# Turning q and k of two batches by DMA transfers, sine tables at the start, and a new order, in a fused attention and gated-convolution kernel

## The chip, the cores and the metric

The kernel runs on one core of one Trainium2 chip. The metric is the device time of one execution in microseconds; for the kernel before it is 174.66 us, the median of three runs (173.97, 174.66, 174.69). A profile of one execution shows the engines: PE is TensorE (matmuls; PEld its weight loads), DVE VectorE, ACT ScalarE, POOL GpSimd, SP SyncE. POOL and SP mainly issue DMA transfers here.

## The reference

Two blocks run one after the other on 4 batches, 8 heads, 768 positions and 64 values per head. The first is attention in which a query sees the 96 latest keys and the first 8, with a bias that grows with distance; the second takes its output as x.

```python
scores = scale * np.matmul(q, k.transpose(0, 1, 3, 2))
is_global = pos[None, :] < 8
is_local = (rel >= 0) & (rel < 96)
bias = -slopes[:, None, None] * dist[None, :, :]
scores = np.where(is_global | is_local, scores + bias, -1e9)
a = softmax(scores)                      # over the keys
x = np.matmul(a, v)                      # then (batch, seq, 512)

proj = x @ w_proj                        # 512 -> 3 * 512
x1, x2, x3 = split(proj)
X2 = np.fft.rfft(x2, n=S, axis=1)
H = np.fft.rfft(filter_fft, n=S, axis=0)
x2_conv = np.fft.irfft(X2 * H, n=S, axis=1)
out = (x1 * x2_conv * x3) @ w_out
```

## The kernel before

Attention of one batch has 7 key tiles of 128 rows (8 global keys and 120 others) and 6 query tiles of 128 rows, each row holding all 8 heads (512 values, fp16). The loads give q and k with positions on the partitions (`qn`, `kn`); the score matmuls need the head's 64 values on the partitions, so every tile is turned: `turned` (line 633) does four 128x128 transposes on PE per tile (line 640) into a PSUM bank and one copy out of it (line 306, on ACT or DVE) into `QT` or `KT`. Batches 1 to 3 turn two tiles per bank, batch 0 one; batch 0's queries are turned from fp32 by `turned32` (line 621). There is one `qn`, one `kn`, one `QT` and one `KT` for all batches. `v` has two buffers.

Work on keys goes in three groups, `GRP` = tiles (0,1), (2,3), (4,5,6), called c0 to c2. For each group and each pair of heads `scores` (line 658, matmuls in line 680) writes PSUM, ACT takes the exp (line 694), and from batch 1 on DVE multiplies a mask (line 711). `values` (lines 729 and 734) multiplies by v, DVE normalises (line 753), `transpose_x` (line 774) turns the result, and `gate` (line 843) makes x1 and x3.

`conv` does the rest of the second block: projections to x2 (line 910), a Fourier transform written as matmuls (line 614) with sine tables `fwd`, the product with the filter's spectrum on DVE, the inverse transform (line 935 and 938) and the output matmul (line 962), whose result SP stores (line 970).

The sine tables come from `tables` (line 408): PE makes angles from a row of indices (`angles`, lines 442 to 449), ACT and DVE reduce them to one turn, and ACT takes the sine (line 427). The rows of indices are made by POOL (`irow`, line 379) and cast by DVE (`rows`, line 384). Sine and exp are in different ACT tables, so a switch between them loads a table. In this kernel the sines wait for all exps of batch 0 and for the masks.

Loads of q, k and v are cast from fp32 to fp16 in transfer and are issued by POOL (line 322), in one queue, except batch 0's q, which SP loads in fp32. SP also issues small copies inside `kn` and `vn` that put the global rows in front of each tile.

Nothing is scheduled by the compiler: `graph` lists all operations with what they read and write, numbered in the order of their creation, and the string `ORDER` gives the sequence in which they are written out, each with its engine (P, A, V, G for POOL, S for SP) and its PSUM banks. A word such as `i26b1` puts 26 dummy matmuls there (`busy`, line 302). Each engine and each queue runs its own part of the sequence in order, waiting for what an operation needs.

Of the kernel before, what the change touches and what calls it, by code (L numbers as in the profile page):

```python
# [16 lines left out]
P = 128  # L17
# [22 lines left out]
0V 8V 31V 11V 7V 12V 1V 10V 9V 17S 50S 15S 16S 48S 49S 58S 18G 5G 39A 35A 42A 43A 45A 41A 6A 47A 37A 32A 2A  # L40
38A 36A 33A 46A 51A 19G 22G 23V 28A 40A 44A 26V 55G 24G 71V 72A 77A 34A 79A 52V 25V 61G 54G 59G 60G i26b1 80P0
86P1 87V 81V 29V 259G 20G 21G 57G 67G 56G 62G 3G i2b3 89P2 90V 27V 30V 88V 53V 13V 261S 260G 64G 63G 65G 257G
256G 258G 68G 66G 70G 69G 82P3 83A 84P4 85A 74A i3b1 109P5 110A 75A 115P3 116V i1b0 91P67 92A 93P01 94A 113P2
114V 269G 270G 267G 268G 273G 263G 95P45 96A 78A 161P6 111P7 112V 157P3 158V 162V 14V 97P01 98A 119P45 120A
123P23 124A 121P67 122A 159P0 160V 262S 265S 264S 275G 274G 276G 279G 277G 266G 271G 155P1 156V 104P45 105V
106V 4V 117P23 118A 167P01 168A 165P67 166A 163P45 164A 99P23 100V 101V 215P0 216A 76A 107P1 108V 130P67 131V
132V 125P23 126V 127V 217V 218V 169P45 170A 73A 102P1 103A 220P6 360P7 488G 490S 272G 495G 133P2 134A 219A
221A 128P3 129V 176P45 177V 178V 361V 171P01 172V 150P3 152V 173V 222V 223V 140P2 142A 356P4 357A 179P5 180V
135P7 358P3 359A 224A 137A 174P2 175V 209V 226V 201V 202V 151P4 153A 154V 204V 371P01 365P23 366A 372A 145P5
147V 208V 203V 210V 211V 205V 206V 196P4 227P6 232A 146P7 148A 149V 234V 230V 235V 212V 207V 213V 236V 237V  # L50
225V 373V 214V 136P5 138A 198A 182P2 192P3 194A 368P01 369A 362P45 363A 197P7 199A 191P3 141P0 143A 228A 231A
193A 229A 233A 144V 238V 370V 195V 298P1 285P0 286A 281P7 282A 184A 386P6 387A 299A 498G 499G 294P0 295A 384P7
385V 239V 367V 139V 283P3 284A 186P6 188A 394P45 395A 397P01 398A 430P7 431V 289P2 290V 364V 181P3 309P6 310A
183A 432P7 433V 240V 396V 503G 504G 278G 489G 492G 485G 486G 502G 497G 487G 388P45 389A 391P01 392A 434P2 435V
390V 491S 505G 501G 496G 187P6 189A 296P7 297A 379P45 380V 381V 436P23 437A 374P01 375V 399V 376V 393V 720G
247P6 248A 439P45 440A 441V 438V 307P7 308A 287P2 288A 241P3 442P01 443A 405P45 406V 190V 407V 242V 382P6 383A
243P7 244A 302P2 303A 400P01 401V 402V 377P6 378V 444V 445P45 446A 447V 408P7 245P3 246A 300P2 301A 249P01
251A 409A 250V 403P6 404A 253P45 254A 255A 304V 292V 448P23 449V 450A 185V 453P01 454V 291V 455V 293V 252V
200V 311V 312V 722S 493S 729G 426P7 420P6 421P4 415P5 417A 422A 423A 411P0 413A 410P1 584P5 585A 456P6 457V
305V 660P4 661A 588P0 589V 306V 717G 713G 735G 716G 718S 494S 714G 313P2 314A 317P3 451P5 452A 412A 318A 479V  # L60
478V 425P6 614P2 615A 727G 734G 506G 726G 280G 732G 662P0 719S 721S 464P4 466A 428A 427A 586P1 587V 414V 612P5
613V 481V 480V 725G 508G 724G 658P3 730G 500G 715G 728G 731G 733G 723G 507G 736G 321P2 322A 663A 323P4 324A
327P1 328V 429V 482V 659V 424V 483V 474P7 476A 319P2 320A 469P0 471A 599P45 600A 590P67 591A 325P2 315P1 316A
326A 473P0 475V 484V 329V 330V 331V 522P3 523A 625P45 596P67 597A 598V 622P01 623A 624V 468P2 526P3 527A 470A
626A 509P6 510V 592V 332V 333V 524P7 525A 616P01 593P23 594A 617A 511P6 512V 601V 595V 336V 513P7 514A 664P45
665A 619P23 667P01 668A 620A 458P6 460V 477V 337V 459P7 461A 517P4 416P5 418A 518A 607P01 602P23 603V 608V
419V 604V 609V 621V 618V 334V 666V 335V 627V 515P7 516A 535P5 536A 530P6 531A 350P4 351A 537P5 812P7 813A
353P6 354A 673P23 674A 538A 670P01 671A 463P4 465A 528P7 529A 842P6 843V 628P23 629V 462V 630V 675V 672V 344P5
610P6 611A 345A 816P4 890P7 605P2 606A 817A 633P01 634V 635V 669V 520V 539V 519V 533V 472V 347P6 348A 631P5
886P3 636P2 637A 887A 632A 891A 341P4 676P01 677V 814P6 815A 342A 681P23 682V 540V 678V 532V 683V 467V 534V  # L70
521V 840P5 841A 644P7 888P6 889A 646A 648P4 650A 653P5 655A 679P0 680A 643P1 645V 847P67 848A 821P45 822A
684P2 547P0 548V 685V 823V 706V 849V 707V 649P3 651A 555P6 556A 549P7 550A 853P01 827P45 828A 898P23 899A
545P6 546A 854A 338P7 339V 708V 340S 349S 352S 355S 346S 343S 638P4 640A 551P5 552A 541P2 553P3 554V 709V 710V
711V 543P6 544A 542A 557V 558V 712V 559V 702P7 818P01 819A 850P45 851A 687P6 639P3 641A 689A 642V 900V 820V
560V 652V 561V 564V 754P2 755A 704A 741P4 742A 844P01 845A 846V 829V 824P23 825A 826V 565V 562V 901P67 902A
739P5 740A 737P4 738A 750P0 892P23 895P67 896A 893A 751A 686P1 688A 752P5 692P4 694A 753A 763P2 743P3 765P0
766A 835P67 836V 837V 563V 903V 697P4 654P1 656A 764A 767V 894V 852V 897V 745P0 746A 699A 744A 578P5 758P1
756P2 757A 759A 856P67 857V 647V 855V 696P4 698A 566P3 567A 579A 568S 580S 830P01 831V 832A 858V 768V 747V
691P4 693A 909P23 910V 761V 581P5 582A 861P67 862V 863A 911V 748V 904P01 905V 749V 906V 760V 575P4 701P2 833P3
834V 657V 912P5 859P6 860A 913A 569P7 838P0 839V 762V 703V 864P6 865A 570A 571S 583S 907P1 908A 934V 935V 936V  # L80
937V 695V 938V 939V 940V 773P3 572P5 573A 774A 769P0 781P6 775P1 777P5 783P7 784A 776A 771P2 772A 782A 778A
770A 867P3 872P7 874A 869A 779P2 780A 785V 786V 700V 787V 788V 690V 789V 790V 791V 792V 958P1 954P0 955A 576A
959A 577S 574S 945P5 946A 941P3 942A 915P0 943P2 944A 969P6 970A 956P1 957A 947P7 948A 882P3 949P2 950A 917A
951V 919P4 967P1 968V 952V 971V 953V 972V 962P5 960P2 961A 884A 877P6 871P7 873A 963A 965V 964V 705V 966V 793V
876P2 866P3 868A 879A 870V 881P7 986P5 990P3 973P0 974A 991A 987A 794P6 977P1 978A 979P0 980V 988P3 989A 975P5
976A 883A 981V 875V 885V 982V 929P1 992P3 993A 878A 795A 994V 995V 983V 984V 996V 997V 985V 796S 800P5 801A
797P0 798A 799S 802S 914P7 916A 918V 999V 998V 880V 1001V 1002V 1000V 803P5 804A 805S 925P6 809P7 810A 811S
920P5 922A 931A 806P0 807A 927A 921A 1014V 1012V 923V 1013V 808S 924P5 926A 928V 1006P7 1007A 1008S 930P6 932A
933V 1015V 1009P4 1010A 1011S 1003P5 1004V 1005S 1022P4 1023V 1024S 1016P7 1017V 1018S 1019P6 1020A 1021S
# [108 lines left out]
class Fused:  # L198
# [10 lines left out]
    Q32 = True  # L209
    LATER = ()  # L210
# [26 lines left out]
    def buffers(self):  # L237
# [9 lines left out]
        self.KT = t("KT", [P, 4, 7 * P])  # L247
# [42 lines left out]
        self.irow = self.X.bitcast(I32).rearrange("p a b -> p (a b)")[0:1, 512:1152].rearrange("p (a b) -> p a b", a=5)  # L290
# [81 lines left out]
    def setup(self):  # L372
# [4 lines left out]
        g.op("A", 0.2, lambda _: nc.scalar.activation(self.warm, self.warm, Act.Exp),  # L377
             r=["warm"], w=["warm"], table="exp", bias=-4000)
        def irow(_):
            p.iota(self.irow[:, 0:4], pattern=[[1, 4], [6, P]], base=0, channel_multiplier=0)  # L380
            p.iota(self.irow[:, 4], pattern=[[1, P]], base=0, channel_multiplier=0)
        g.op("G", 0.8, irow, w=["irow"], bias=-1975.0)

        def rows(_):
            v.memset(self.one, 1.0)
            for j in range(3):
                v.memset(self.cst[:, j:j + 1], 192.0 * (j + 1))
            v.tensor_copy(self.row, self.irow)
        g.op("V", 0.8, rows, r=["irow"], w=["rows"], bias=-1970)
# [18 lines left out]
    def tables(self):  # L408

        nc, g, S = self.nc, self.g, self.S  # L410
        exps = [x for x in g.ops if x.name in ("exp", "mask")]
        nf = 2.0 * math.pi / S * (1.0 - 4.0e-7)
        for a, n in enumerate((512, 256)):
            b = g.bank()
            g.op("P", 0.5 if a == 0 else 0.3, lambda _, a=a, b=b: self.angles(a, b.f32()),
                 r=["rows"], acq=[b], after=[x for x in exps if x.name == "exp"][7:8], name="angles")
            th = self.th[a]
            g.op("A", act(n), lambda _, th=th, b=b, n=n: nc.scalar.activation(
                th, b.f32()[:, 0:n], Act.Copy, bias=MAGIC, scale=1.0 / S), use=[b],
# [189 lines left out]
    def forward(self, ss, src, key, bs):  # L609
        def run(_):  # L610
            for s, b in zip(ss, bs):
                i, terms = 0 if s in (0, 1, 4) else 1, self.TERMS[s]
                for n, (f, t) in enumerate(terms):
# [4 lines left out]
                      ("fwd", a) for s in ss for a in ((0, 2) if s < 4 else (1,))])  # L618


    def turned32(self, t):
        nc, g = self.nc, self.g
        b = g.bank()

# [602 lines left out]
```

## Time and profile before

| what | value |
|---|---|
| median of three runs | 174.66 us |
| the profiled execution, its own time | 174.67 us |
| its span, first to last instruction | 172.9 us |
| PE busy | 166.8 us (96%) |
| DVE busy | 158.4 us (92%) |
| ACT busy | 151.9 us (88%) |
| POOL busy (issuing transfers included) | 75.8 us (44%) |
| granted TensorE clock | 1.0 of full speed |
| turns of q and k, line 640 | 184 matmuls, 9.8 to 100.4 us |
| table loads of ACT | 3, of 1.28 us |

The span starts with the first instruction. Busy times are unions, so an engine that works on two overlapping matmuls counts once; the length that a group gives for a matmul runs from its start to its modelled end and is longer than the distance between two matmuls. A wait is put down to what released it.

### The profile page before, as it was taken

The page shows a single profiled execution, that of the slowest core. Times are in us where ns is not written, and L with a number is a line of the kernel's source. Part 1 is how long each engine was busy: PE and PEld are TensorE (multiplying, and loading weights), DVE is VectorE, ACT ScalarE, POOL GpSimd, SP SyncE. Part 2 cuts the span into 40 slices and gives each one's busy share as a digit, 9 for nine tenths or more (in the row PEclk, how much of TensorE's full clock was granted, in tenths as well). Part 3 has the DMA queues.
Part 4 walks back from the last instruction along what each step waited for, and adds up shares of the span by engine and source line. Part 5 has one row for each costly group of instructions (what it writes and reads, how often), then busy time and mean ns, then how long its engine had stood idle before and what let it go on. Part 6 is the DMA issues. An engine that isn't in the chain of part 4 may idle for free.

```text
span 172.9 us, 4486 instructions
## 1 busy us (share of the span) xinstructions
PE 166.8 (96%) x1732; PEld 106.1 (61%) x1732; DVE 158.4 (92%) x352; ACT 151.9 (88%) x305; POOL 75.8 (44%) x97
## 2 busy tenths in 40 slices
PE   7998999999999999999999999999999999999990
PEld 2374988655665668764657867645577755574530
DVE  6869969999999999999999999999989999989970
ACT  2999899999999999999999999999797897678821
POOL 7999998629989964999760000000000000000000
PEclk9999999999999999999999999999999999999999
DMA  4999999999999996999999000720030303003554
GB/s 86 188 198 166 168 171 177 207 184 153 154 161 145 153 148 50 126 147 175 152 151 57 4 0 4 272 91 0 4 121 6 121 2 121 4 0 151 213 205 161
DMA packets 91133, 20.74 MB, mean 120 GB/s; under 512 B 83864, under 2 KB 88040, under 8 KB 91112
## 3 DMA queue, kind: packets, MB, share of 16 engines
q0 software_dynamic: 80912, 12.14, 96.6%
q1 hardware_dynamic: 10200, 8.31, 15.3%
q8 instruction: 13, 0.21, 0.5%
q14 instruction: 8, 0.07, 0.1%
HBM read 25.84 MB, written 6.29 MB: 186 GB/s over the span
## 4 chain that ended last, share of the span: by engine, by line
PE 93%; DVE 4%; issue 0%; ACT 0%; ACTq 0%; DVEq 0%
PE bank L843 25%; PE bank L910 12%; PE bank L962 12%; PE bank L614 6%; PE bank L680 6%; PE bank L640 6%; PE bank L935 5%; PE bank L302 5%; PE bank L729 4%; PE bank L774 4%; PE bank L734 3%; PE bank L671 2%; PE bank L938 1%; DVE KT L306 1%; DVE vn L1097 1%; DVE vn L306 1%
## 5 line engine op out<-in xcount | busy, mean ns | idle before, releaser
L843 PE MATMUL bank<-xT,w 128*128 128x384 f16 x256 | 48.7, 326 | 0.0
L694 ACT ACTIVATE E<-bank 128x864 f16<-128x864 f32 x48 | 40.6, 902 | 1.3 <-PE bank L680 1.3
L843 PEld LDWEIGHTS <-w 128*128 128x128 f16 x256 | 23.4, 98 | 15.6 <-issue 0.7
L322 POOL DMA_DIRECT2D kn<-in_k_dram x28 | 25.7, 921 | 10.7 <-PE bank L640 4.3
L322 POOL DMA_DIRECT2D vn<-in_v_dram x28 | 25.6, 921 | 1.7 <-DMA wo<-in_moe_w_out_dram 1.1
L962 PE MATMUL bank<-wo,y 128*128 128x512 f16 x96 | 23.8, 379 | 0.0
L711 DVE TENSOR_TENSOR E<-E,mask 128x864 f16<-128x864 f16 x36 | 20.6, 600 | 0.0
L322 POOL DMA_DIRECT2D qn<-in_q_dram x18 | 16.3, 918 | 0.3 <-issue 0.2
L753 DVE TENSOR_TENSOR xn<-bank,rc 128x512 f16<-128x512 f32 (+1 forms) x21 | 16.1, 771 | 0.3
L853 ACT CAST g<-bank 128x384 f16<-128x384 f32 x32 | 15.4, 512 | 1.1 <-PE bank L843 0.9
L310 ACT ACTIVATE ot<-bank 128x512 f32<-128x512 f32 x20 | 11.9, 611 | 4.9 <-PE bank L962 4.9
L729 PE MATMUL bank<-vn,E 128*128 128x65 f16 x224 | 15.2, 193 | 0.0
L729 PEld LDWEIGHTS <-E 128*128 128x128 f16 x224 | 14.0, 97 | 1.8
L734 PE MATMUL bank<-vn,E 128*128 128x65 f16 x192 | 14.9, 193 | 0.0
L306 ACT CAST eo<-bank 128x384 f16<-128x384 f32 x28 | 12.7, 512 | 1.7 <-PE bank L938 0.9
L680 PE MATMUL bank<-QT,KT 64*128 64x216 f16 (+2 forms) x224 | 14.0, 241 | 0.0
L306 ACT CAST X<-bank 128x512 f16<-128x512 f32 x22 | 12.7, 613 | 1.3 <-PE bank L614 1.2
L962 PEld LDWEIGHTS <-y 128*128 128x128 f16 x96 | 8.8, 98 | 8.1
L310 ACT ACTIVATE ab<-bank 128x512 f16<-128x512 f32 x22 | 12.8, 619 | 1.1 <-PE bank L910 1.0
L310 ACT ACTIVATE x<-bank 128x384 f16<-128x384 f32 x26 | 13.1, 523 | 0.8 <-ACT g L853 0.4
L734 PEld LDWEIGHTS <-E 128*128 128x128 f16 x192 | 13.1, 97 | 0.7
L680 PEld LDWEIGHTS <-KT 64*128 64x128 f16 x224 | 8.5, 94 | 6.6 <-issue 5.0
(144 smaller groups left out, 369.3 us busy)
## 6 DMA issues: line engine op xcount, KB each, us to landing
out_dram<-ot SPq DMA_DIRECT2D x24, 256.0 KB
kn<-in_k_dram POOLq DMA_DIRECT2D x28, 120.0 KB, 6.3
vn<-in_v_dram POOLq DMA_DIRECT2D x28, 120.0 KB, 6.4
qn<-in_q_dram POOLq DMA_DIRECT2D x18, 128.0 KB, 6.5
ot<-in_q_dram SPq DMA_DIRECT2D x6, 256.0 KB
w<-in_moe_w_proj_dram POOLq DMA_DIRECT2D x4, 256.0 KB, 7.3
g<-in_moe_filter_fft_dram POOLq DMA_DIRECT2D x1, 768.0 KB, 11.0
w<-in_moe_w_proj_dram POOLq DMA_DIRECT2D x1, 512.0 KB, 12.7
```

What stands on the lines that cost most here:

```text
L306: {"A": nc.scalar.copy, "V": nc.vector.tensor_copy, "G": nc.gpsimd.tensor_copy}[e](out, in_)
L310: self.nc.scalar.mul(out, in_, c)
L322: return self.g.op(eng, 0.57 + 0.00035 * nbytes[0] if eng == "G" else 0.5, lambda _: e.dma_start(dst, src), w=w, r=r, nbytes=nbytes, name= ...
L680: nc.tensor.matmul(bs[hh].f32()[:, off:off + w], self.KT[hs, hp, P * m:P * m + P], self.QT[hs, hp, KL * m:KL * m + w], start=(off == 0 and ...
L694: g.op("A", act(864), lambda _: nc.scalar.activation(eo, bs[0].two()[:, :, 0:432].rearrange("p h (m w) -> p h m w", m=2), Act.Exp, scale=s ...
L711: g.op("V", dve(864, 2), lambda _: nc.vector.tensor_mul(eo, eo, mk), r=[("mask", 2 * hp), ("mask", 2 * hp + 1)], w=[("E", hp, gi)], name=" ...
L729: nc.tensor.matmul(o[:, n, hh], ef[:, at:at + P], vt[:, t, 2 * hp + hh, 0:D + 1], start=first, stop=(t == 0), skip_group_check=True)
L734: nc.tensor.matmul(o[:, n, hh], ef[:, at:at + P], vt[:, t - 1, 2 * hp + hh, 0:D + 1], start=False, stop=True, skip_group_check=True)
L753: nc.vector.tensor_mul(to, o[:, :, :, 0:D], rc.to_broadcast([P, 2, 2 * nt, D]))
L843: nc.tensor.matmul(bk.f32()[:, 0:h], self.w[:, c, o + P * j:o + P * j + P], self.xT[:, c, h * s:h * s + h], start=(c == 0), stop=(c == 3))
L910: nc.tensor.matmul(bk.f32(), src[:, c], w[:, c, DM:2 * DM], start=(c == 0), stop=(c == 3))
L962: nc.tensor.matmul(bk.f32(), y[:, c, P * t:P * t + P], self.wo[:, c, :], start=(c == 0), stop=(c == 3))
```

## The change

- `crossed` is new and takes the place of `turned` for batches 2 and 3 (`CROSS`). For each group SP issues one transfer with `transpose=True` for all key tiles of the group (2, 2 or 3 tiles), and one per query tile: 3 + 6 per batch, 18 in all, from `kn` to `KT` and from `qn` to `QT`. No PE, PSUM, ACT or DVE takes part.
- `KT` is laid out with the tile index ahead of the head pair, so that a group of tiles is one stretch; the score matmuls read it accordingly, and readiness of `QT` is kept per head pair.
- `tables` is called right after `setup`; the sines no longer wait for the exps, and exps and masks wait for the sines. The first dummy activation uses the sine table.
- The rows of indices are made by DVE: a row 0 to 127 by doubling (one memset, seven adds), then four multiples of it; POOL's two iotas and the cast are gone.
- `ORDER` is new as a whole. It has 29 dummy matmuls in place of 32. In it SP's queue has batch 2's transfers after the two small copies of batch 1 in `vn`, with batch 2's small copies in `kn` after the first of them; batch 3's transfers stand ahead of most of batch 0's stores. PE runs batch 1's last scores, then projections, transforms and values, then batch 2's first scores.

```diff
+    CROSS = (2, 3)
...
-        self.KT = t("KT", [P, 4, 7 * P])
+        self.KT = t("KT", [P, 7, 4, P])
...
-        g.op("A", 0.2, lambda _: nc.scalar.activation(self.warm, self.warm, Act.Exp),
-             r=["warm"], w=["warm"], table="exp", bias=-4000)
-        def irow(_):
-            p.iota(self.irow[:, 0:4], pattern=[[1, 4], [6, P]], base=0, channel_multiplier=0)
-            p.iota(self.irow[:, 4], pattern=[[1, P]], base=0, channel_multiplier=0)
-        g.op("G", 0.8, irow, w=["irow"], bias=-1975.0)
-
+        g.op("A", 0.2, lambda _: nc.scalar.activation(self.warm, self.warm, Act.Sin),
+             r=["warm"], w=["warm"], table="sin", bias=-4700)
         def rows(_):
+            row = self.row
+            v.memset(row[:, 4, 0:1], 0.0)
+            for n in (1, 2, 4, 8, 16, 32, 64):
+                v.tensor_scalar(row[:, 4, n:2 * n], row[:, 4, 0:n], float(n), None, op0=Alu.add)
+            for j in range(4):
+                v.tensor_scalar(row[:, j], row[:, 4], 6.0, float(j), op0=Alu.mult, op1=Alu.add)
             v.memset(self.one, 1.0)
             for j in range(3):
                 v.memset(self.cst[:, j:j + 1], 192.0 * (j + 1))
-            v.tensor_copy(self.row, self.irow)
...
             g.op("P", 0.5 if a == 0 else 0.3, lambda _, a=a, b=b: self.angles(a, b.f32()),
-                 r=["rows"], acq=[b], after=[x for x in exps if x.name == "exp"][7:8], name="angles")
+                 r=["rows"], acq=[b], name="angles", bias=-4600)
...
-                 r=[("th", a)], w=[("fwd", a)], table="sin", name="sines", after=exps)
+                 r=[("th", a)], w=[("fwd", a), "sin"], table="sin", name="sines", bias=-4600)
...
+    def crossed(self, c):
+        g, sync = self.g, self.nc.sync
+        ts = self.GRP[c]
+        n = len(ts)
+        dst = self.KT[:, ts[0]:ts[0] + n].rearrange("p t i c -> p (t i) c")
+        src = self.kn[:, ts[0]:ts[0] + n].rearrange("p t h d -> p (t h d)")
+        g.op("S", 0.6, lambda _: sync.dma_start(dst, src, transpose=True), nbytes=(512 * n, 256), name="cross",
+             r=[("kn", t) for t in ts] + [("kz", t) for t in ts], w=[("KT", t) for t in ts])
+        for t in ([0, 1, 2], [3, 4], [5])[c]:
+            g.op("S", 0.6, lambda _, t=t: sync.dma_start(
+                self.QT[:, :, P * t:P * t + P], self.qn[:, t].rearrange("p h d -> p (h d)"), transpose=True),
+                nbytes=(512, 256), name="cross", r=[("qn", t)], w=[("QT", t, i) for i in range(4)])
...
-                                     self.KT[hs, hp, P * m:P * m + P],
+                                     self.KT[hs, m, hp],
...
-            scale=self.scale), use=bs, w=[("E", hp, gi)], table="exp", name="exp")
+            scale=self.scale), use=bs, r=["sin"], w=[("E", hp, gi)], table="exp", name="exp")
...
-            for what, ts, buf in (("q", new, self.qn), ("k", self.GRP[c], self.kn)):
+            if b in self.CROSS:
+                self.crossed(c)
+            for what, ts, buf in () if b in self.CROSS else (("q", new, self.qn), ("k", self.GRP[c], self.kn)):
...
         self.setup()
+        self.tables()
         self.load_first()
...
-        g.batch = (-10.0, 0.0)
-        self.tables()
```

## The prediction

> **What bounds the kernel now.** I began with the page's table of busy time and its strip of 40 slices (4.32 us each), to see which engine has nothing left to give and when.
>
> ```profile
> PE 166.8 (96%) x1732; PEld 106.1 (61%) x1732; DVE 158.4 (92%) x352; ACT 151.9 (88%) x305; POOL 75.8 (44%) x97
> ...
> PE   7998999999999999999999999999999999999990
> ...
> DMA  4999999999999996999999000720030303003554
> ```
>
> TensorE is full from the second slice to the last but one; VectorE and ScalarE are nearly full. The DMA engines are full too, up to slice 21 (95 us), with one dip, and then almost idle. Next the chain that ended last, its summary and some pieces (start, length, what):
>
> ```profile
> PE 93%; DVE 4%; issue 0%; ACT 0%; ACTq 0%; DVEq 0%
> ...
> 1.20 8.29 PE bank L302 x26
> ...
> 48.91 0.45 PE bank L640 x8
> ...
> 164.14 4.33 PE bank L962 x20
> 168.55 0.60 ACT ot L310
> ```
>
> 93% of the span is TensorE's own work, so a matmul taken out between 9.5 us (end of the 26 dummy matmuls) and 168.5 us shortens the kernel by its pitch, as long as TensorE is not made to wait instead. Line 640 is the turning of q and k: eight turns in 0.45 us, 0.056 us each (the 219 ns that the groups give is one turn's length in the pipeline, not its pitch). The windows of 5 us say that the middle has no slack on the other two engines (window, length, busy of PE, PEld, DVE, ACT, POOL, then clock, DMA share, GB/s):
>
> ```profile
> 50.00:55.00 5.00, 5.00 (x62) 2.75 (x60) 4.95 (x13) 4.98 (x8) 4.59 (x6) 1.00 2.26 147
> 95.00:100.00 5.00, 5.00 (x85) 3.87 (x83) 4.93 (x12) 5.00 (x10) 0.00 (x0) 1.00 0.01 3
> ```
>
> Last the queues that the change uses: SP's first loads and small copies (timeline), POOL's waits, and the time from issue to landing of the k loads.
>
> ```profile
> 1.81 7.44 SPq L322 DMA_DIRECT2D ot<-in_q_dram  x5
> 17.68 2.90 SPq L322 DMA_DIRECT2D kn<-kn  x2
> 51.38 1.48 SPq L322 DMA_DIRECT2D kn<-kn  x2
> ```
>
> ```profile
> POOL kn L322 <- PE bank L640: 4.3, 2, 4.0
> POOL kn L322 <- PE bank L843: 3.2, 1, 3.2
> ```
>
> ```profile
> DMA to landing us min/median/max: 3.9/6.3/12.2
> ```
>
> One kn buffer serves all batches, so POOL's next loads wait until the old tiles are turned (4.0 us once, at 63 us).
>
> **The change, part by part.** The sum is made against the profiled execution: span 172.9, its own time 174.67, which is the median (174.66) to 0.01.
>
> Turns removed: batches 2 and 3 lose 6 q tiles and 7 k tiles of 4 turns each, 2 x 52 = 104 x 0.056 = 5.8 us of TensorE, all inside the full stretch (65 to 101 us). Taken: -5.8.
>
> Copies removed: 16 moves out of PSUM, 11 on ScalarE and 5 on VectorE in the old order. By rows of 1.03 us (1024 wide) and 0.59 (512) on ScalarE, 0.69 and 0.42 on VectorE, about 10 and 2.5 us. Off the path, but this lets TensorE keep the gain: without it, engines that are 4.9 of 5 busy would hold up a faster TensorE. The new order spends the relief: it hands ScalarE some 12 further evacuations of VectorE's (xT, X, h, ot), so I expect VectorE near 152 and ScalarE near 148 busy.
>
> Angles and sines first: the angle matmuls (0.43 us from 23.4, 0.37 from 26.28) leave the full stretch for the time of the dummies: -0.8. One of three ACT table loads goes (1.28 us each, at 3.1, 28.5 and 33.9); at 28.5 ScalarE was full, so that is relief and not path. POOL loses two iotas (0.79 us); VectorE gets 12 small instructions instead, by rows of 0.06 to 0.17 us about 1.2 us, ahead of its first memsets, against the 0.55 us cast that goes.
>
> The start: the 26 dummies become 6, the angles, and 9. The first 13 of the old ones took about 0.43 us each (1.2 to 6.3 us), the rest 0.21. So 6 x 0.43 + 1.6 (angles at the slow pitch) + 2.3 for the nine, from 1.2 us: the first turn could begin at 7.6 instead of 9.3, if the q tile is there, which no row shows, as TensorE was covered until 9.49; I count half, -0.8. Behind it stand 14 dummies instead of 6: +8 x 0.21 = 1.7 if they cover no wait. ScalarE ahead of its first exp: 14.0 us of work by its rows (16 slopes 3.0, two table loads 2.6, near copies 2.0, inverse tables 1.35 and so on), from about 1.9 us, so the first exp near 15.9 instead of 14.12; but it then has no sine work and no further table load left at 28 to 35 us. Taken for the start: +0.9; bounds -1.5 (nothing waits) and +4 (1.8 us of later exp and 1.7 of dummies, both in full).
>
> The crossbar transfers: 18 on SP, 9 per batch. No row of this kernel shows one. What they must do is clear: SP waits until batch 1's last scores have read QT and KT, issues q tile 2, two small kn copies, q tiles 0 and 1, then k tiles 0 and 1; only then can batch 2's first scores run. In the new order TensorE has between these two points 6 projections (0.86), 6 forward transforms, 6 of the filter's, 6 value groups, 5 turns of x and 2 gates (0.65): 15.8 us by the rows. For batch 3 the like count gives 14.7. Price: nearest row, SP's q loads, 5 x 1024 packets of 256 B in 7.44 us with POOL's loads beside them: 1.5 us per 1024. A q tile is 512 such rows (0.75), k tiles 0 and 1 1024 (1.5). The chain is 0.75 + 2 x 0.69 + landing + 1.5 + landing (the other q tiles hide under the copies' landing). With 3.9 us to land: 11.4; with 6.3: 16.2; with the longest, 12.2: 28. I take the middle of the first two, 13.8: no wait. Ends: 0 late, and 28 - 15.8 + 28 - 14.7 = 25 us late.
>
> Behind the waiting transfers on SP stand, for batch 2, the two vn copies, which values want 20 us later; for batch 3, the stores of batch 0, which in the old kernel began only at 108.6 us. POOL's next k load now waits for a transfer where it waited 4.0 us for line 640; the transfers also add 104 x 128 = 13312 packets, 19 us of DMA time at the q loads' pace, to engines that are full until 95 us. Their cover is that batch 3's k and v are wanted from about 96 and 115 us, TensorE's position in the new order. Taken 0; ends -2 (POOL's 4 us wait gone) and +6.
>
> [...]
>
> Sum: 174.67 - 5.8 - 0.8 + 0.9 = 169.0.
>
> **Rivals.** *Transfers late* (slower). For: the DMA engines are full in the first window, a landing has taken 12.2 us, and SP issues in order. Against: 15 us of cover twice. It decides from a chain of 18.6 us ((15.8 + 14.7 + 6.6) / 2, 6.6 being the gain without the start); at 22 us per chain it costs 6.2 + 7.3 and gives 182.5.
>
> *The start is longer.* For: ScalarE's 14 us before its first exp, 8 more dummies. Against: the old start left ScalarE idle until 3.1 us and POOL carries less. 3 us more than I take: 172.0; it would have to be 4.8 more (173.8) to hide the change from a measurement, and the bound above is 3.1.
>
> *The DMA engines become the bound for batch 3.* Loads that ended at 95 us end near 112 if the 19 us are added whole; k tile 5, nearly last in POOL's order, is wanted at about 105. Late by some 4: 173. Against: only half of the transfers fall while POOL still loads, and its old stall of 4 us is room.
>
> **Chances.** Forecast 0.52 (167.0 to 171.5); late transfers 0.24 (176 to 190); longer start 0.12 (171 to 175); DMA bound 0.12 (171 to 176). Half a per cent, 0.87 us, is about what a measurement tells from no change: faster is below 173.8, which takes the forecast and some two thirds of the last two cases, 0.68; the same 0.08; slower 0.24. The range 166.5 to 179.0 leaves out most of the late transfers and a little below.
>
> **What would show it.** Line 640 falls to 80 turns and TensorE's busy time by 6 to 9 us (dummies included); no wait of TensorE longer than 1 us on KT or QT before batch 2's and 3's first scores; transfers on SP at 0.7 to 1.5 us each; two table loads, both before 17 us; DMA full until about 105 us. The prediction is wrong if TensorE stands before those scores, if SP spends several us on each transfer, or if the first exp comes after 18 us.

## The result, and the profile after

The changed kernel takes 180.88 us in the median (180.18 to 181.81), against 174.68 us for the kernel before: a ratio of 1.0365, interval 1.0335 to 1.0395. It is 6.2 us slower where I had forecast 5.7 us faster, and it lies above the upper end of my range, 179.0. The profiled execution took 181.81 us, its span 180.0. A run more than 1.5% above the fastest of its kernel is left out of the ratios below; this concerns a single run, and the text says where.

The page's busy times and strips of the changed kernel (40 slices of 4.5 us):

```profile
PE 164.2 (91%) x1625; PEld 100.9 (56%) x1625; DVE 153.7 (85%) x346; ACT 150.2 (83%) x306; POOL 76.1 (42%) x95
...
PE   6987599999999999999999881999999999999991
...
DMA  6999999999999999999999999920001110400754
```

TensorE now has two holes, at 9 to 23 us and at 99 to 113 us, and the DMA engines stay busy to 117 us (the end of the 26th slice) instead of 95 us; the last of it are stores. TensorE's busy time fell by only 2.6 us although 5.8 us of turns are gone; by the account below, work at a lower clock gave back 2.9 us.

The chain that ended last, its summary and its long pieces (start, length, what):

```profile
PE 51%; DMA 27%; DVE 12%; ACT 4%; issue 3%; POOL 1%; SPq 1%; POOLq 0%; DVEq 0%; ACTq 0%
...
59.38 9.13 DMA KT<-kn
...
81.42 10.06 DMA qn<-in_q_dram
...
92.96 12.83 DMA qn<-in_q_dram
...
107.10 5.46 DMA KT<-kn
```

TensorE's share of the chain fell from 93% to 51%, and 27% are DMA: loads of q and v (19%) and transfers of k (8%). They follow each other: a k transfer of batch 2 lets POOL go on, POOL's loads of batch 3 come in late, the last q tile lands at 105.8 us, and only then can its transfer, and the last k transfers behind it on SP, be made. SP's queue shows the same (start, length with waiting, line, operation):

```profile
51.98 1.30 SPq L629 DMA_TRANSPOSE QT<-qn  x1
...
83.49 5.95 SPq L629 DMA_TRANSPOSE QT<-qn  x2
...
93.01 3.18 SPq L626 DMA_TRANSPOSE KT<-kn  x1
96.28 10.71 SPq L629 DMA_TRANSPOSE QT<-qn  x2
...
109.93 2.40 SPq L626 DMA_TRANSPOSE KT<-kn  x1
```

A q transfer's issue takes 1.24 us there in the median of twelve; the pair at 96.28 takes 10.71, because the source of its second has not landed (a q load that ended at 105.79, the transfer began at 105.81). The waits (total, times, longest):

```profile
POOL kn L322 <- DMA KT<-kn: 7.7, 1, 7.7
...
PE bank L693 <- DMA KT<-kn: 5.6, 3, 4.0
DVE inr L312 <- ACT inv L310: 3.8, 1, 3.8
```

The first line is POOL standing in order behind a k transfer that still reads the buffer it wants to load. The second is TensorE standing before batch 3's scores. The third belongs to the start: VectorE stands for ScalarE's copy of the inverse tables, with batch 0's k copies behind it. Five windows of 5 us (busy of PE, PEld, DVE, ACT, POOL, then clock, DMA share, GB/s):

```profile
15.00:20.00 5.00, 2.48 (x28) 1.45 (x28) 1.51 (x5) 4.96 (x9) 5.00 (x6) 1.00 2.18 141
20.00:25.00 5.00, 4.79 (x44) 3.15 (x44) 3.31 (x7) 2.48 (x4) 5.00 (x7) 0.66 2.21 141
...
100.00:105.00 5.00, 3.85 (x45) 2.36 (x42) 3.54 (x9) 3.96 (x9) 0.90 (x1) 1.00 1.90 121
105.00:110.00 5.00, 3.57 (x37) 2.63 (x34) 4.86 (x9) 3.67 (x8) 0.00 (x0) 1.00 2.53 142
110.00:115.00 5.00, 2.40 (x14) 1.29 (x15) 1.87 (x5) 1.67 (x2) 0.00 (x0) 0.83 1.04 206
```

Each hole is followed by a stretch at a lower granted clock, 0.66 and 0.83. An account of the span from these windows: 172.9 before; -5.8 for the turns and -0.8 for the angles, as predicted; +3.7 of TensorE standing at 10 to 35 us (20.85 busy against 24.52 before) and +1.6 for the clock of 0.66 there (4.79 x 0.34); +0.7 standing at 60 to 70 us; +5.2 at 100 to 115 us (9.81 busy of 15) and +1.3 for the clock of 0.83 at 110 to 120. That is 178.7 of the 180.0 measured; 1.3 us I could not place.

### The profile page after: what moved, and what is told of

Its sections match the earlier page's. It is cut to its first block, busy times and chain, and to the rows that moved or that the text cites. A ratio compares the mean times of both kernels' runs of the same rounds, so it can differ in the third digit from the quotient of the medians.

```text
span 180.0 us, 4283 instructions
## 1 busy us (share of the span) xinstructions
PE 164.2 (91%) x1625; PEld 100.9 (56%) x1625; DVE 153.7 (85%) x346; ACT 150.2 (83%) x306; POOL 76.1 (42%) x95
## 4 chain that ended last, share of the span: by engine, by line
PE 51%; DMA 27%; DVE 12%; ACT 4%; issue 3%; POOL 1%; SPq 1%; POOLq 0%; DVEq 0%; ACTq 0%
PE bank L856 15%; DMA qn<-in_q_dram 13%; PE bank L977 9%; DMA KT<-kn 8%; PE bank L925 6%; DMA vn<-in_v_dram 6%; PE bank L693 4%; PE bank L684 3%; PE bank L950 3%; PE bank L613 2%; PE bank L652 2%; PE bank L742 2%; PE bank L787 2%; PE bank L747 2%; DVE eo L383 1%
## 5 line engine op out<-in xcount | busy, mean ns | idle before, releaser
L856 PE MATMUL bank<-xT,w 128*128 128x384 f16 x256 | 50.0, 333 | 0.0
L707 ACT ACTIVATE E<-bank 128x864 f16<-128x864 f32 x48 | 41.4, 897 | 9.1 <-PE bank L693 8.2
L856 PEld LDWEIGHTS <-w 128*128 128x128 f16 x256 | 23.7, 100 | 15.8 <-issue 2.1
L693 PE MATMUL bank<-QT,KT 64*128 64x216 f16 (+2 forms) x224 | 14.6, 245 | 5.6 <-DMA KT<-kn 5.6
L310 ACT ACTIVATE ot<-bank 128x512 f32<-128x512 f32 x22 | 13.3, 611 | 3.8 <-PE bank L977 3.4
L742 PE MATMUL bank<-vn,E 128*128 128x65 f16 x224 | 15.9, 193 | 0.3 <-DVE xn L766 0.2
L306 ACT CAST X<-bank 128x512 f16<-128x512 f32 x24 | 13.9, 605 | 2.4 <-PE bank L613 2.4
L742 PEld LDWEIGHTS <-E 128*128 128x128 f16 x224 | 14.5, 97 | 2.6 <-issue 0.2
L747 PE MATMUL bank<-vn,E 128*128 128x65 f16 x192 | 15.6, 193 | 0.0
L310 ACT ACTIVATE ab<-bank 128x512 f16<-128x512 f32 x23 | 13.7, 616 | 1.0 <-PE bank L925 0.8
L747 PEld LDWEIGHTS <-E 128*128 128x128 f16 x192 | 13.3, 97 | 1.3 <-issue 0.3
L306 ACT CAST eo<-bank 128x384 f16<-128x384 f32 x27 | 12.0, 506 | 1.0 <-PE bank L953 0.7
```

The lines of the kernel that those rows point to most:

```text
L306: {"A": nc.scalar.copy, "V": nc.vector.tensor_copy, "G": nc.gpsimd.tensor_copy}[e](out, in_)
L310: self.nc.scalar.mul(out, in_, c)
L693: nc.tensor.matmul(bs[hh].f32()[:, off:off + w], self.KT[hs, m, hp], self.QT[hs, hp, KL * m:KL * m + w], start=(off == 0 and not near), st ...
L707: g.op("A", act(864), lambda _: nc.scalar.activation(eo, bs[0].two()[:, :, 0:432].rearrange("p h (m w) -> p h m w", m=2), Act.Exp, scale=s ...
L742: nc.tensor.matmul(o[:, n, hh], ef[:, at:at + P], vt[:, t, 2 * hp + hh, 0:D + 1], start=first, stop=(t == 0), skip_group_check=True)
L747: nc.tensor.matmul(o[:, n, hh], ef[:, at:at + P], vt[:, t - 1, 2 * hp + hh, 0:D + 1], start=False, stop=True, skip_group_check=True)
```

## The experiments

### The start

In the changed kernel's order, ScalarE's last mask goes behind the copies of the inverse tables, and two of VectorE's copies of them go behind batch 0's k copies.

```diff
 ScalarE:
-  mask 3, inverse tables, first exp
+  inverse tables, mask 3, first exp
 VectorE:
-  inverse tables 2 and 3, k copies of batch 0
+  k copies of batch 0, inverse tables 2 and 3
```

> The changed kernel with three words of its order moved: ScalarE's first mask (and with it the load of the exp table) goes behind the last of ScalarE's inverse-table copies, and VectorE's two last inverse-table copies go behind its next k copies. Theory A (the start lost its time to VectorE standing 3.8 us for ScalarE's inverse-table copy, with the k copies behind it, so that TensorE stood 2.4 us and its clock fell to 0.66): 177.5 to 178.8 us, no wait of TensorE over 1 us on KT before 24 us. Rival B (the start is set by ScalarE, whose first exp comes at 18.3 us whatever VectorE does): 180 to 181 us, TensorE idle as long as before between 15 and 25 us.

Measured: 181.7 us, 1.0444 (1.0373 to 1.0515) of before, so nothing is gained on the changed kernel. Windows of this run:

```profile
20.00:25.00 5.00, 4.82 (x81) 3.80 (x80) 4.14 (x5) 5.00 (x8) 5.00 (x7) 1.00 2.24 148
...
105.00:110.00 5.00, 1.19 (x12) 0.62 (x10) 4.13 (x9) 1.30 (x4) 0.00 (x0) 1.00 2.18 140
```

The start is mended in large part: TensorE is busy 8.94 us of 15 to 25 us instead of 7.27, and at full clock, though from 10 to 35 us it is still busy 2.2 us less than in before. But now it stands 3.8 us of the five at 105 us. TensorE came sooner to a place where it has to wait for batch 3's tiles anyway (5.5 us at a stretch, for a k transfer). The start is a real loss of the change, but not the one that sets the end.

### The transfers without the new start, and the new order without transfers

The kernel before with its own start and order; the turns of batches 2 and 3 leave, and nine transfers per batch stand on SP behind the last scores of the batch before.

```diff
+    CROSS = (2, 3)
...
-            for what, ts, buf in (("q", new, self.qn), ("k", self.GRP[c], self.kn)):
+            if b in self.CROSS:
+                self.crossed(c)
+            for what, ts, buf in () if b in self.CROSS else (("q", new, self.qn), ("k", self.GRP[c], self.kn)):
```

> The kernel before, with its old order and start, but batches 2 and 3 turned by the 18 transfers, which SP issues as soon as the scores of the batch ahead are through. Theory E (the DMA engines become the bound: they are full until 95 us and the transfers add 19 us or more): batch 3's first scores, at 102.8 us before, find their tiles late by 4 to 9 us and the kernel takes 173 to 178 us. Rival F (the transfers fit under the old order's cover, the loss of the changed kernel is its start and its order): 168 to 170 us, no wait on KT or QT over 1 us.

Measured: 181.11 us, 1.0378 (1.0328 to 1.0427). The transfers alone cost as much as the whole change, and more than either theory expected. TensorE stands at 65 to 75, 85 to 95 and 105 to 115 us here; POOL stood 10.3 us for a k transfer:

```profile
POOL kn L322 <- DMA KT<-kn: 10.3, 1, 10.3
```

The other half, the changed kernel's order with the turns back on TensorE, each just ahead of its scores:

```diff
-    CROSS = (2, 3)
+    CROSS = ()
...
```

> The changed kernel with the turns of batches 2 and 3 back on TensorE, ahead of their group's first scores in the new order; POOL's next loads wait for the turns. Theory C (the transfers cost what TensorE lost at 100 to 120 us): 5.8 us of turns come back, 5.2 us of standing at 100 to 115, 0.7 at 60 to 70 and some 1.5 us of slow clock go: 179 to 180 us, no standing after 30 us. Rival D (the new order has the gap whatever turns the tiles): the gap stays and the turns come on top, 184 to 187 us. If the start alone were to blame for all, this would be near 181.

Measured: 201.96 us, 1.1593 (1.1536 to 1.165). This says nothing on the question: I had put the turns so late that POOL stood 11.6 and 7.4 us for them and all loads of batch 3 came late. What the new order would be worth by itself stays open.

### What a transfer costs by itself

Two kernels hold nothing but loads, transfers and copies, with VectorE separating the stages.

```diff
+        nine()
+        nine_seen()
+        gate()
...
+        loads(range(14))
+        nine()
+        nine_seen()
+        loads_seen(14)
+        gate()
```

> Leaves out the whole computation and stores zeros: only transfers, a stage at a time, each stage seen by VectorE before the next starts. A q tile, two k tiles and three k tiles turned alone; three k tiles copied without a turn; the nine transfers of a batch alone; 14 loads alone; 14 loads with the nine; 14 loads with copies of the nine's bytes. [...] Theory H (a transfer costs about what a copy of its rows costs, and it is the full DMA engines that make it late): three k tiles 3 to 6 us, the nine 10 to 16 us, and 14 loads with the nine take about the sum of both, 13 + 12 = 25 us or more, whether turned or copied. Theory I (only turning collides with the loads): with plain copies the last stage is at least a quarter shorter than with turns.

Measured: one q tile alone takes 1.31 us on SP and is seen by VectorE after 2.5 us, two k tiles after 3.0, three after 3.6 (a plain copy of those three after 2.6). The nine of a batch take 14.4 us alone, 14 loads 16.0 alone, both together 25.8. The last stage, loads beside copies, had the stores in it and could not be read; so a second kernel:

> Leaves out the whole computation and stores near zeros: the nine transfers of a batch alone, copies of the same bytes alone, 14 loads alone, 14 loads with the nine, 14 loads with the copies, each stage over before the next. Known from the run before: 14.4 us for the nine alone, 16.0 for 14 loads, 25.8 for both. Theory H (the bytes count, turned or not): loads with copies end 8 to 11 us after loads alone. Theory I (turning is what collides): loads with copies end under 5 us later than loads alone, and the copies alone take under 8 us.

The windows of its stages: the nine, the same bytes as plain copies, 14 loads, 14 loads with the nine, 14 loads with the copies (second number: length; then busy of DVE and POOL, clock, DMA share, GB/s):

```profile
15.94:30.33 14.39, 0.23 (x1) 0.00 (x0) 1.00 0.60 118
30.87:38.77 7.90, 0.28 (x2) 0.00 (x0) 1.00 0.60 216
39.80:55.57 15.77, 0.00 (x0) 12.25 (x14) 1.00 1.83 116
56.28:81.59 25.31, 0.47 (x3) 12.25 (x14) 1.00 1.71 140
82.30:103.08 20.78, 0.95 (x3) 12.25 (x14) 1.00 1.66 170
```

Beside nine turned transfers 14 loads take 9.5 us longer, beside the same bytes copied 5.0 us. Beside loads the nine are seen after 24.2 us instead of 14.4. So a turned transfer costs here about twice what a copy costs, alone (14.4 against 7.9 us) and beside loads (9.5 against 5.0), between what the two theories expected. A plain copy of the same bytes is also far fewer packets (1296 against 6432 in a pair of runs below); no run copies in as many packets, so whether the turning or the number of packets makes the difference stays open.

### Which batch

The transfers of one batch alone, in before's order. First batch 3, whose transfers fall behind most of the loads:

```diff
-    CROSS = (2, 3)
+    CROSS = (3,)
...
```

> The kernel before, old order and start, with batch 3 alone turned by nine transfers, issued when batch 2's last scores are through (about 90 us), when most loads have landed. Theory E (what decides is whether the DMA engines are full): most of the nine run beside few loads, about 15 us by the run with transfers alone, from 90 us to 105, against first scores at 102.8 minus the turns: late by 2 to 5 us, gain 2.9, so 174 to 177. Rival F (transfers fit): 171.5 to 172.5.

Measured: 173.24 us, 0.992 (0.9888 to 0.9952), between the two theories. Then batch 2, whose transfers fall among batch 3's loads:

```diff
-    CROSS = (2, 3)
+    CROSS = (2,)
...
```

> The order, the tables and the start of before; only batch 2's queries and keys go by the nine transfers, batch 3 is turned on TensorE. The mirror of the run with batch 3 alone (173.24 us). Theory D (the DMA engines are full as long as loads are left): the nine stand among batch 3's 20 loads, each set of 14 loads grows by 9.5 us beside nine transfers, so loads that ended at 94 us in before end at 100 to 104, batch 3's turns on TensorE wait for their tiles, and the time is 176 to 180 us although TensorE has 52 turns (2.9 us) less to do. POOL stands over 5 us for a k transfer. Rival T (what costs is the transfer as such, its latency and SP's serial issue): the same as for batch 3 alone, 172 to 174 us.

Measured: 178.73 us, 1.0254 (1.0228 to 1.028). The same nine transfers gain 1.3 us in one place and lose 4.1 in the other, so it is not the transfer as such. POOL's first k load of batch 3 in before's timeline:

```profile
67.32 0.91 POOL L322 DMA_DIRECT2D kn<-in_k_dram  x1 [4.00 <-PE bank L640]
```

The same load in the second run, two of its waits, and three windows:

```profile
72.80 0.91 POOL L322 DMA_DIRECT2D kn<-in_k_dram  x1 [10.02 <-DMA KT<-kn]
```

```profile
POOL kn L322 <- DMA KT<-kn: 10.0, 1, 10.0
...
PE bank L978 <- DMA wo<-in_moe_w_out_dram: 3.5, 1, 3.5
```

```profile
65.00:70.00 5.00, 3.71 (x37) 2.56 (x35) 4.90 (x10) 3.38 (x9) 0.00 (x0) 1.00 2.17 129
...
85.00:90.00 5.00, 1.45 (x16) 0.64 (x13) 4.65 (x12) 2.19 (x5) 3.17 (x4) 0.99 1.94 184
90.00:95.00 5.00, 5.00 (x32) 2.53 (x32) 0.97 (x2) 2.48 (x4) 4.94 (x6) 0.67 2.41 152
```

POOL stands until 72.8 us (67.3 in before), and the output weight, 9 issues further on, comes too late for TensorE. With 2.9 us of turns saved, the transfers of batch 2 cost some 7 us in all, and the windows hold about that: 1.8 us of standing at 65 to 75 us, 3.5 at 85 to 90 for the output weight, and 1.7 for the clock of 0.67 behind it. The time is what theory D expected, but loads that take longer, its reason, do not show here: they landed after 5.9 (k), 6.2 (v) and 6.5 us (q) in the median, against 6.3, 6.4 and 6.5 in before. They were issued later, not delivered more slowly.

### Moving the loads

Three runs tried to keep both batches' transfers and to spare the loads. In the changed kernel, POOL loads batch 3's last q and k tiles ahead of its v:

```diff
 POOL:
   q b3 t3,
+  q b3 t4, k b3 t3, k b3 t6, k b3 t5,
   v b3
```

> The changed kernel with four words of POOL's order moved: the last q tile and three k tiles of batch 3 are loaded ahead of all of batch 3's v tiles but none of batch 2's. Theory J (TensorE stood at 100 to 115 us because the last q and k tiles of batch 3 were the last that the full DMA engines delivered, the q tile landing at 105.8): these land 7 to 9 us earlier, the standing there falls from 5.2 to under 2 us and the slow clock behind it goes, 174 to 176 us. Rival K (the transfers themselves are slow beside the loads, whatever they wait for): the v loads still collide with them, and the kernel gains under 2 us, 179 to 181.

Measured: 178.93 us in the median of four runs (177.52 to 181.01), 1.0224 (1.0148 to 1.0301) of before without the slowest, between the two theories. In the profiled run, the one of 177.52 us, TensorE's standing at 100 to 115 us fell from 5.2 to 1.3 us; POOL still stood 10.0 us. Then with POOL's standing filled by loads that need no turned buffer, and with the mended start:

```diff
 POOL:
+  v b2 t4, t0, t3, t5, t2, wo,
   k b3 t0,
   q b3 t3,
+  q b3 t4, k b3 t3, k b3 t6, k b3 t5,
   v b3
```

> The changed kernel with order alone mended at three places: POOL issues batch 2's other v loads and the output weights in the 7.7 us in which it stood for the first k transfer; then batch 3's q and k ahead of its v; and the start as in the run with the moved mask. Theory L (the loss is where transfers and loads were put in POOL's and SP's queues, not the transfers): no standing over 1 us after 30 us, so the 6.6 us of turns and angles come through against a start some 3 us longer, 170 to 173 us, under the kernel before. Rival M (the DMA engines cannot carry loads and transfers by the time that the new order wants them): standing of 4 us or more remains between 60 and 120 us, 176 to 180.

Measured: 179.44 us, 1.0309 (1.0257 to 1.0362). POOL no longer stands for a transfer, but 5.7 and 4.6 us for landings of its own v and k loads, and TensorE is busy 1.82 us of the five at 100 us. Last, before's order with both transfers and only the output weight moved:

```diff
 POOL:
+  wo,
   k b3 t1,
   k b3 t2,
-  wo,
   k b3 t5
```

> Before's order with both batches by transfers (181.11 us), with one move: the output weight is loaded ahead of batch 3's first k tile, where POOL stood 10.3 us for a transfer. Theory Q (POOL's queue in order: what stands behind the waiting load is late, the output weight first): TensorE no longer stands at 85 to 95 us, and the time is 175 to 177.5 us. Rival M (the DMA engines cannot carry loads and transfers in time, whichever comes first): the standing moves to batch 3's tiles at 95 to 112 us and the time stays at 179 to 182 us.

Measured: 182.99 us, 1.048 (1.0446 to 1.0514). TensorE's wait for the output weight is gone, POOL's standing is 12.2 us, and TensorE stands 10.5 us between 65 and 80 and between 90 and 115 us: 5.6 of them before scores that want transferred tiles, 3.7 before products with v for which the profile names no cause. Whatever is loaded first, something else is late.

### The two causes taken apart

Batch 2's transfers do two things: they load the DMA engines, and they make POOL stand. First the load alone: before, with nine added transfers that nobody waits for.

```diff
...
+            x = g.op("S", 0.6, lambda _, dst=dst, src=src: sync.dma_start(dst, src, transpose=True),
+                     nbytes=(512 * n, 256), name="beside", r=[("w", j) for j in range(4 * n)],
+                     w=[("beside", a, i)], after=g.readers.get(("ot", a), ()))
...
```

> Before, with nothing taken away: batch 2 and 3 are turned on TensorE as before. Added are nine turned transfers by SP (six of one tile, three of two, 12 of the 13 tiles of a batch), which read the projection weight and write spare space that nobody reads, each issued once the tile of batch 2 that it stands for has landed. So TensorE, POOL and the buffers wait for none of them; they only use the DMA engines and SP. Theory D (the DMA engines' load by itself makes the loads late): batch 3's loads end 4 to 6 us later than in before, its turns on TensorE wait, and the time is 176 to 179 us. Rival Q (what costs is that POOL stands in order behind a transfer, and TensorE waits for it): 174 to 175.2 us, as before.

Measured: 180.57 us, 1.0347 (1.0308 to 1.0385): 5.8 us for transfers that nobody reads. They started at 52.39 us, since the order they were put in made no wait for the tiles; so they stood beside batch 2's last loads as well. That is 7 us earlier than batch 2's own in the run with batch 2 alone (59.28), and about when they start in the changed kernel (51.98). SP took 18.66 us to issue the nine; batch 2's small k copies stand ahead of them (50.80 us), so SP's queue is not what held its turns. A piece of the chain that leads to TensorE's hole, and two windows:

```profile
61.09 13.87 DMA qn<-in_q_dram
```

```profile
65.00:70.00 5.00, 4.57 (x61) 3.74 (x59) 4.83 (x11) 5.00 (x11) 2.01 (x3) 1.00 1.78 139
70.00:75.00 5.00, 1.27 (x12) 0.84 (x12) 2.05 (x4) 2.08 (x4) 2.73 (x3) 0.94 1.77 154
```

A q load of batch 2 landed after 13.87 us; the median of all 18 q loads of the kernel was 9.3 us, in before 6.5. TensorE stood 4.2 us before the turns of late q and k tiles, then ran at a clock of 0.72 in the next window. The same bytes not turned:

```diff
-            x = g.op("S", 0.6, lambda _, dst=dst, src=src: sync.dma_start(dst, src, transpose=True),
+            x = g.op("S", 0.6, lambda _, dst=dst, src=src: sync.dma_start(dst, src),
```

> The same as the nine turned transfers that nobody waits for, but as plain copies of the same tiles, not turned. Theory D with the measured prices (14 loads grow by 9.5 us beside turned transfers and by 5.0 us beside copies): about half of what the turned ones cost over before, 175.2 to 177 us. If only the turning disturbs the loads: as before, within 0.5 us. If any added traffic on the DMA engines costs as much: the same as the turned ones.

Measured: 174.4 us, 0.999 (0.9974 to 1.0006): nothing. SP issued the nine copies in 6.86 us; they added 1296 packets, the turned ones 6432. I had expected half the cost. The copies delay the loads too: the 18 q loads landed after 8.2 us in the median. But TensorE did not stand for them: it was busy 5.00 us of five in every window from 50 to 115 us. So the copies' price was hidden, not absent.

Then the standing alone. The first try put POOL's load of batch 3's first k tile behind batch 2's first scores in the written order:

```diff
...
-                  f"load{what}{t}")
+                  f"load{what}{t}", after=[self.held] if what == ("kn",) and b == 3 and t == 1 else [])
...
```

> Before, no transfers, with one wait added: POOL's first load of a k tile of batch 3 waits until batch 2's first scores (73.4 us in before's trace; in before POOL stood until 67.3 us there, and in the run with batch 2 alone by transfers until 72.8 us). Everything behind it on POOL, the output weight too, is 6 us later. Rival Q: TensorE stands for the output weight at 85 to 90 us and for batch 3's tiles, and the time is 177 to 180 us, most of the cost of batch 2's transfers. Theory D: 174 to 175.5 us, since the loads had room.

Measured: 174.69 us, 0.9998 (0.9976 to 1.002), but the trace shows the load at 67.45 us as in before (67.32): the edit made no wait, and the run tells nothing on the question. The second try made the scores read the buffer:

```diff
+            if hold:
+                nc.tensor.matmul(bs[0].f32()[:, 0:8], self.kn[:, 1, 0:2, :].rearrange("p h d -> p (h d)"),
+                                 self.ident[:, 0:8], start=True, stop=True, skip_group_check=True)
...
```

> Before, no transfers, and POOL held for good: batch 2's first scores (73.4 us in before's trace) also read batch 3's first k place by a matmul of 8 columns that the scores then overwrite, so that POOL's first k load of batch 3 starts behind them, 6 us later than in before (67.3 us) and as late as in the run with batch 2 alone by transfers (72.8 us). Rival Q (POOL's standing alone makes most of the cost of batch 2's transfers): TensorE stands for the output weight at 85 to 90 us and for batch 3's tiles, 177 to 180 us. Theory D (it is the load on the DMA engines; loads on free engines catch up): 174 to 175.5 us.

Measured: 180.03 us, 1.03 (1.0231 to 1.0368). POOL's timeline and three windows:

```profile
74.03 0.91 POOL L322 DMA_DIRECT2D kn<-in_k_dram  x1 [10.94 <-PE bank L685]
```

```profile
70.00:75.00 5.00, 5.00 (x61) 3.98 (x59) 5.00 (x12) 5.00 (x12) 0.96 (x2) 1.00 0.01 3
...
85.00:90.00 5.00, 2.74 (x35) 1.51 (x33) 4.90 (x12) 3.56 (x7) 4.58 (x6) 1.00 1.22 140
90.00:95.00 5.00, 3.42 (x15) 1.84 (x16) 2.35 (x5) 1.00 (x2) 3.27 (x4) 0.68 2.38 153
```

While POOL stands the DMA engines are idle (a share of 0.01, 3 GB/s, from 70 to 75 us), and the queue does not make that up: POOL issues a load every 0.9 us, and this one starts 6.7 us later than in before. TensorE stands 3.8 us at 85 to 95 us, for the output weight, and runs at a clock of 0.68 there. So POOL's standing costs 5.5 us by itself, by the same hole before the output weight as in the run with batch 2's transfers alone, and it makes most of their 7 us. The load on the DMA engines can cost as much, 5.8 us, without any standing of POOL for a transfer, when the transfers start as early as in the changed kernel; its hole, at 70 to 75 us before turns of batch 2, is not one of the run with batch 2's transfers alone. How the loss of the changed kernel divides between the two no run shows.

### Batch 3 alone, with the loads rearranged

Before's order with batch 3 alone by transfers, and POOL's loads rearranged: batch 2's last v tiles and the output weight ahead of batch 3's first k tile, the rest of batch 3's v last.

```diff
+    CROSS = (3,)
...
 POOL:
+  v b2 t4, t6, t2, t5, wo,
   k b3 t1, q b3 t0,
-  v b3 t5,
   k b3 t0, q b3 t1, k b3 t3,
-  v b3 t4, v b2 t4,
   k b3 t2,
-  wo,
   k b3 t5, q b3 t4, q b3 t3, q b3 t5, q b3 t2,
-  v b3 t2,
   k b3 t4, k b3 t6,
+  v b3 t5, t4, t2,
   v b3 t1, t6
```

> The run with batch 3 alone by transfers (173.24 us), with POOL's loads in another order: batch 2's last v tiles and the output weight ahead of batch 3's first k tile, all of batch 3's q and k tiles ahead of the rest of its v. Theory D: the nine can be issued at once behind batch 2's last scores, SP's pair of 8.65 us at 83 us is gone, the idle TensorE of 1.4 us between 90 and 110 us goes, and the time is 171.5 to 172.8 us, about 1% to 1.8% under before. Rival B (behind 85 us the stretch is bound by VectorE and the evictions, not by the tiles' arrival): 173 to 174 us, no different from batch 3 alone.

Measured: 172.89 us, 0.9902 (0.9884 to 0.992), 1% under before and just above the 171.5 to 172.8 that I expected. SP's first pair of q transfers of batch 3, first in the run with batch 3 alone, then here:

```profile
83.19 8.65 SPq L630 DMA_TRANSPOSE QT<-qn  x2
```

```profile
82.63 2.63 SPq L630 DMA_TRANSPOSE QT<-qn  x2
```

TensorE still loses 0.4 us between 90 and 105 us, and the 2.9 us of turns became 1.7 in the median. Without the transfers, the new order of the loads alone:

```diff
-    CROSS = (3,)
...
```

> Before without any transfer, with only the order of POOL's loads from the run of 172.89 us (batch 2's last v tiles and the output weight ahead of batch 3's first k tile, the rest of batch 3's v last). If that run's gain of 1.7 us over before is the transfers' (52 turns of TensorE after the loads are over): this one is at 174.2 to 175 us, as before. If the gain is the loads' order: 172.5 to 173.5 us.

Measured: 174.86 us, 1.0015 (1.0003 to 1.0028). The order of the loads gains nothing by itself; the gain comes only with the transfers.

## Why the prediction was wrong

**The step that failed** is the last paragraph on the transfers: "Taken 0; ends -2 and +6" for POOL's wait and the 19 us of DMA time. The end of +6 was near to what one batch's transfers cost, 7.0 us, but I chose 0, with the argument that batch 3's k and v are wanted only from about 96 and 115 us. Three things were wrong with that cover.

First, I counted POOL's old wait of 4 us as room that the transfers would use or free. It grew instead: 7.7 us here, 10.0 to 12.2 in before's order. It had little slack behind it: with the DMA engines idle, a start 6.7 us later made TensorE stand 3.8 us for the output weight and cost 5.5 us. I looked at when the loads are used and not at POOL's pace of 0.9 us per issue, by which a late queue stays late, nor at the output weight that stands in it.

Second, I priced the transfers' packets as if they shared the engines evenly, and then set them against the cover of batch 3 alone. What they do to a load that is on its way beside them is more: 9.5 us on 14 loads, q loads landing after 9.3 instead of 6.5 us in the median, one of them after 13.87, and 5.8 us of time for transfers that nobody waits for. This depends on where they stand: in before's order with all 18 transfers and the output weight moved, the loads landed after 6.4 (k), 6.6 (v) and 6.7 us (q), near before's 6.3, 6.4 and 6.5, and POOL's standing of 12.2 us is what the trace shows there. At the q loads' pace half of 13312 packets is 9.7 us, so the size was right and the place for it wrong.

Third, behind its holes TensorE ran at a lower clock, 0.66 and 0.83. The prediction has no such term; it cost 1.6 and 1.3 us here.

**The chain of transfers, "13.8: no wait", was longer, and its cover nearly held.** From SP's first transfer of batch 2 (51.98 us) to the landing of its first k tiles (68.51 us) it took 16.5 us, a little over the 16.2 that I had for landings of 6.3 us and over the 15.8 of cover; TensorE waited 0.45 us for it. For batch 3 it took some 20.5 us (83.49 to 104.0), because SP stood for source tiles that had not landed; TensorE waited 1.2 us for its first k tiles and 4.0 us for the next ones, and that belongs to the step above. Landings of the loads were 7.1 (k), 8.6 (v) and 9.4 us (q) in the median, and my 3.9 to 6.3 were those of a kernel without transfers.

**The start, "+0.9; bounds -1.5 and +4", was mis-sized.** The first exp came at 18.32 us, 2.4 later than the 15.9 I worked out. ScalarE had 14.9 us of work ahead of it, with a third table load, where I had 14.0, and it stood 2.1 us for the angle matmuls, a wait that my sum did not have. The price in TensorE's time was 5.3 us with the clock, above my bound of +4, whose two terms in fact add up to 3.5. The reason is an order that my sum of ScalarE's work did not hold: a mask and its table load stood ahead of a copy that VectorE waited for. Mended, it did not shorten the kernel, as long as batch 3's tiles were late.

**The turns, -5.8, were right in size and became gain only where the loads were over**: 1.3 to 1.7 of 2.9 us for batch 3. VectorE and ScalarE came out near 153.7 and 150.2, where I had 152 and 148.

**The rivals.** *The DMA engines become the bound for batch 3* named the mechanism, with "loads that ended at 95 us end near 112", and the DMA share falls from 2.53 to 1.04 at 110 us; it priced it at 173 us for want of the clock, the start and POOL's queue. *Transfers late* gave 182.5 us, near the measured time, by another way: chains of 22 us each that make TensorE stand 6.2 and 7.3 us before the first scores. They took 16.5 and 20.5 us, and it stood 0.45 and 1.2 us there; that the totals are close is chance.

**The signs.** Line 640's 80 turns came true; TensorE's busy time fell by 2.6 and not by 6 to 9 us. Of the three signs that I had set against myself, all came: TensorE stood before batch 3's scores, SP spent several us on a transfer, and the first exp came after 18 us. ACT loaded three tables before 17 us (0.74, 6.82 and 15.78), not two.

## What to carry to other kernels

The nine transfers of batch 2 took 2.9 us of turns off a full engine and were paid for on the queues they touched: POOL stood 10.0 us for a buffer that one of them still read, and TensorE 3.5 us for the output weight behind it in POOL's queue. So ask which buffer a transfer still reads when the next load wants it, and what stands behind that load in the same queue. POOL's queue, at 0.9 us per issue, did not catch up here: 6.7 us of standing cost 5.5 us at the end, even with idle DMA engines. Look for a place for turned transfers behind the loads; the same nine gained 1.3 us there and lost 4.1 among them.

## What I had not expected of the hardware

- Nine turned transfers that nobody waits for cost 5.8 us (6432 packets), the same bytes copied cost nothing (1296 packets), 174.4 against 174.73 us, although with the copies too the q loads landed after 8.2 us in the median, against 6.5 in before.
- After TensorE stood for 2 to 4 us, the granted clock in the following windows of 5 us was 0.66 to 0.83 in the changed kernel and at its lowest 0.50 to 0.82 in nine of the experiments; in windows of 1 us of the changed kernel it is 0.50 for two at a time (22 to 24 and 114 to 116 us). The profile of before shows 1.0 from the first window to the last in which TensorE works. It is no fixed rule: in the run with the output weight moved, TensorE was busy 2.45 us of the five from 70 us and the clock stayed at 1.0 in that window and the next two; in the changed kernel it stood 2.4 us until 20.2 us and the clock fell to 0.66. In the run with POOL held, the hole of 3.8 us and what followed it cost 5.5 us.
- SP's issue of a q transfer takes 1.24 us in the median in the changed kernel, twice a plain copy's 0.6 in the second kernel of transfers alone, where the issues of the nine took 11.7 us of SP.
